# Retention and a GELU layer on one core: two chunks per group of small matmuls, and the tails turned by DMA

## The chip, the cores and the metric

One core of a Trainium2 chip runs the kernel. The metric is the device time of one execution in microseconds (us); several executions are taken and their median is compared. The engines have short names in the profile: PE is TensorE (PEld its weight loads), DVE is VectorE, ACT is ScalarE, POOL is GpSimd, and SP is the engine that issues most DMAs here.

## What is computed

There are 8 batches, 8 heads, a sequence of 576 positions and a head width of 64; the layer after it has 4608 rows, 512 inputs and 2048 hidden columns.

```
scores = scale * q @ k^T
Dmat   = gamma[h] ** (i - j) where i >= j, else 0
attn   = (scores * Dmat) @ v
x      = attn as [batch * 576, 8 * 64]
h      = x @ w_in
g      = 0.5 * h * (1 + tanh(c * (h + 0.044715 * h**3)))
out    = g @ w_out
```

Inputs and output are fp32; the kernel multiplies in fp16 and sums in fp32.

## The kernel before

**Retention by chunks.** The decay lets the sequence be cut into 4 chunks of 128 positions and a tail of 64 (called chunk `NC` in the code). For one chunk of one batch PE does the following small jobs. `score` (L304, matmul on L313) makes keys times queries, head by head: 8 matmuls that use 64 of the 128 rows of the array, two of them beside each other; VectorE multiplies the two PSUM banks that result by the causal mask (L319) into `ret`. `state` (L328, L333) makes keys times values, 8 matmuls that use 64 of the 128 columns, two beside each other; VectorE carries the running state on in `scan` (L341) and ScalarE spreads it into block form in `spread` (L351, L354). `av` (L356, L363) makes `ret` times values, again on 64 columns, and adds the part that comes from the chunks before (L381; for a tail L373) on the whole array. `put` (L389) copies the result to `xT` on ScalarE. Chunk 0 has no earlier part. A tail has its heads packed in two halves of the partitions, so it has half as many matmuls.

**The layer.** Rows are handled in 9 stages t of 512 rows: stages 0 to 7 have the four chunks of batch t, stage 8 all tails. From stage 2 on a stage has 30 steps u. Steps 0 to 15 are the up steps (`up`, L403: 4 matmuls of 128x512 and a GELU on ScalarE, through the two `hp` banks). After steps 3, 7, 11 and 15 VectorE makes sums of GELU results (`act_sums`, L480 to L483). Steps 16 to 29 are the product steps: seven products of half size, 1, 6, 5, 7, 2, 3 and 4 in this order, two steps each (`prod`, L485, matmul on L498), with their own banks A, B and C. After each product `after` (L505) adds or copies: product 6 leaves bank B, VectorE makes `u2` from it (L531), and product 7 then goes on summing into the same bank B; in the same way product 3 goes on in bank C once VectorE has read it (L536). Stage 1 has the same 30 steps with up steps in halves.

**Who decides the order.** The program is written in the order in which each engine executes it. `at(t, u, f)` hangs a job behind step u of stage t, and `run` emits it there. So every engine is a queue in program order; an instruction that waits holds back all behind it on its engine.

**Where the small jobs hang before.** `group` (L666) puts the score and the state of one chunk and the values (`av`) of the chunk before behind one step, and `PLAN` (L620) sets the steps: 6, 11, 16 and 21 for the four chunks of batch t+1, and 26 for the tail of batch t-2. Each group thus changes the way in which PE's array is split: whole, 64 rows, 64 columns, whole.

**Turning.** Scores need queries and keys with the head width on the partitions. Up to batch 2 PE does this (`turn`, L275). From batch 3 on `turn_dma` (L293) has SP issue two DMA transposes for a batch, behind step 24 of stage b-2. Before them POOL casts 8 blocks (L253, behind steps 16 to 23), and POOL is held by a copy named `gate` (L704, behind step 16) until the stage's last sums are made. The tails are all turned on PE, 4 matmuls each, with a copy on VectorE (L288). Their loads go over POOL's queue (L83), their casts over POOL (keys, queries) and ScalarE (values, L240).

**PSUM.** Eight banks: two `hp`, the three `att` banks t0, t1, t2 in turn, and A, B, C, which the small jobs may use while the products leave them free.

Of the kernel before, what the change touches and what calls it, by code (L numbers as in the profile page):

```python
# [10 lines left out]
ALU = mybir.AluOpType  # L11
F32 = mybir.dt.float32
# [7 lines left out]
def kernel(  # L20
# [43 lines left out]
    def bank(tag, name, dt=F32):  # L64
        if tag == "att":
            tag = "t" + str(turns["n"] % 3)
            turns["n"] += 1
        return ps.tile([128, 512 if dt == F32 else 1024], dt, tag=tag, name=name, bufs=BUFS[tag])
# [235 lines left out]
    def score(b, c, tag="att"):  # L304
        a = att[b]
        n = HP if c < NC else 2
        w = 128 * n
        d, o = turned(b, c)
        st = [bank(x, "st") for x in (tag if isinstance(tag, tuple) else (tag, tag))]
        for p in range(n):  # L310
            for hl in range(2):
                r = slice(64 * hl, 64 * hl + 64)
                nc.tensor.matmul(  # L313
                    st[hl][:, 128 * p : 128 * p + 128], d[r, 0, o + p, :], tq(b, c, p)[r], start=True, stop=True
                )
        m = cm if c < NC else tm
        for hl in range(2):
            r = sb.tile([128, 512], F16, tag="ret", name="ret", bufs=5)
            nc.vector.tensor_tensor(  # L319
                out=r[:, 0:w], in0=st[hl][:, 0:w], in1=m.rearrange("p n i -> p (n i)"), op=ALU.mult  # L320
            )
            a["ret"][c, hl] = r

# [1 line left out]
        c = c % NC  # L325
        return slice(512 * c + 128 * p + 64 * hl, 512 * c + 128 * p + 64 * hl + 64)

    def state(b, c, tag="att"):  # L328
        a = att[b]
        us = bank(tag, "us")  # L330
        for p in range(HP):
            for hl in range(2):
                nc.tensor.matmul(  # L333
                    us[64 * hl : 64 * hl + 64, 64 * p : 64 * p + 64],
                    a["k"][:, col(c, p, hl)],
                    a["v"][:, col(c, p, hl)],
                    start=True, stop=True,
                )
        a["U"] = us

    def scan(b, c):  # L341
        a = att[b]
        uc = a.pop("U")[:, 0:256].rearrange("p (q d) -> p q d", d=64)
        if c > 0:
            s = sb.tile([128, HP, 64], F32, tag="vs", name="vs", bufs=2)
            nc.vector.tensor_tensor(out=s, in0=uc, in1=a["w"], op=ALU.add)
            uc = s
        a["w"] = w = sb.tile([128, HP, 64], F32, tag="ws", name="ws", bufs=2)
        nc.vector.tensor_tensor(out=w, in0=uc, in1=gt, op=ALU.mult)  # L349

    def spread(b, c, cp, hls=(0, 1)):  # L351
        for hl in hls:
            r = slice(64 * hl, 64 * hl + 64)
            cp(out=(tbd[b % 2][r, c, :, r] if c < NC - 1 else tbt[b % 4][r, :, r]), in_=att[b]["w"][r])  # L354

    def av(b, c, tag="att"):  # L356
        a = att[b]
        n = HP if c < NC else 2
        td = tbd[b % 2]
        xs = bank(tag, "xs")  # L360
        for p in range(n):
            for hl in range(2):
                nc.tensor.matmul(  # L363
                    xs[64 * hl : 64 * hl + 64, 128 * p : 128 * p + 128],
                    act_of(b, "v", c)[:, col(c, p, hl)],
                    a["ret"][c, hl][:, 128 * p : 128 * p + 128],
                    start=(p == 0), stop=True, skip_group_check=True,
                )
        if c == NC:
            for s in range(2):  # L370
                for u in range(2):
                    o = 128 * s + 64 * u
                    nc.tensor.matmul(  # L373
                        xs[:, o : o + 64],
                        tbt[b % 4][:, 2 * u + s, :],
                        tq(b, c, s)[:, 64 * u : 64 * u + 64],
                        start=False, stop=True, skip_group_check=True,
                    )
        elif c > 0:
            for p in range(HP):  # L380
                nc.tensor.matmul(  # L381
                    xs[:, 128 * p : 128 * p + 128],
                    td[:, c - 1, p, :],
                    tq(b, c, p),
                    start=False, stop=True, skip_group_check=True,
                )
        a["xs"] = xs

    def put(b, c):  # L389
        xs = att[b].pop("xs")  # L390
        if c == NC:
            nc.scalar.copy(
                out=xT[:, GM + b].rearrange("p (u s) t -> p s u t", u=2),
                in_=xs[:, 0:256].rearrange("p (s u t) -> p s u t", s=2, u=2),
            )
            return
        src = xs.rearrange("p (n g t) -> p g n t", n=HP, g=2)
        g0 = 8 * (b % 2) + 2 * c
        nc.scalar.copy(out=xT[:, g0 : g0 + 2], in_=src)  # L399
# [170 lines left out]
        "o": (nc.vector.tensor_copy,),  # L570
    }

    CH = range(NC + 1)

    def cc(b, key, c, eng):
        cast(b, key, c, eng)
        pump(int(c < NC))
# [18 lines left out]

    def first(c):
        score(0, c, ST[c % 2])
        state(0, c, ("A", "t2")[c % 2])
        scan(0, c)  # L600

    first(0)
    for c in range(NC):
        if c + 1 < NC:
            cc(0, "k", c + 1, P)
            cc(0, "v", c + 1, P)
            turn(0, c + 1, A.copy, "C")
            spread(0, c, A.copy)
            filler(3, "B")
            first(c + 1)  # L610
        else:
            for g in range(4):
                for ct in range(4):
                    cast_w("i", g, ct)
            spread(0, c, A.copy)
            filler(3, "C")
        av(0, c, "B")
        put(0, c)

    PLAN = {1: zip((8, 13, 18, 23, 27), [(2, c) for c in range(NC)] + [()])}  # L620
    for t in range(2, 7):
        PLAN[t] = zip((6, 11, 16, 21, 26), [(t + 1, c) for c in range(NC)] + [(t - 2, NC)])
    PLAN[7] = zip((2, 7, 12, 17), [(5, NC), (6, NC), (7, NC), ()])
    TAILS = {b: ((b + 2, 5), (b + 2, 15)) for b in range(5)}
    TAILS |= {5: ((6, 16), (6, 24)), 6: ((6, 25), (7, 4)), 7: ((7, 5), (7, 9))}
    gate = const.tile([128, 1], F16, name="gate")
    events = {}

    def at(t, u, f):
        events.setdefault((t, u), []).append(f)  # L630

    def run(t, u):
# [20 lines left out]
    for c in range(NC):  # L653
        at(*CU[c], lambda c=c: (cc(1, "k", c, P), cc(1, "v", c, A if c else P)))
        at(*TU[c], lambda c=c: turn(1, c, A.copy))
        at(*VU[c], lambda c=c: (av(1, c, "AB"[c] if c < 2 else "att"), put(1, c), spread(1, c, A.copy)))
    for c in range(NC):
        at(*SU[c], lambda c=c: (score(1, c), state(1, c), scan(1, c)))
    at(1, 9, lambda: weight_sums(4, "32"))
# [1 line left out]
    at(1, 20, lambda: weight_sums(4, "4"))  # L661


    late = []

    def group(t, u, b=None, c=0):  # L666
        prev = late.pop() if late else None
        if b is not None:
            if b < NPE or c == NC:
                at(t, u - 2, lambda: turn(b, c, V.tensor_copy))  # L670
            at(t, u, lambda: score(b, c))
            if c < NC:
                at(t, u, lambda: (state(b, c), scan(b, c)))
                at(t, u + 2, lambda: spread(b, c, A.copy, (0,)))
                at(t, u + 3, lambda: spread(b, c, A.copy, (1,)))
            late.append((b, c))
        if prev:
            at(t, u, lambda: av(*prev, "C" if u < NF else "hp"))
            at(t, u + 1, lambda: put(*prev))

    def tail_in(t, u, b):
        at(t, u, lambda: load_tail(b))

    def tail_cast(t, u, b):
        at(t, u, lambda: (new_tail(b), [cc(b, key, NC, e) for key, e in zip("kqv", (P, P, A))]))

    for b, (l, k) in TAILS.items():
        tail_in(*l, b)
        tail_cast(*k, b)
    for t, us in PLAN.items():  # L690
        for u, x in us:
            group(t, u, *x)

    for b in range(2, B):
        ent = [(key, c) for c in range(NC) for key in "kqv"]
        eng = {"k": P, "q": P, "v": A}
        if b == 2:
            t0, ut = 1, [1, 1, 2, 6, 6, 7, 11, 11, 12, 16, 16, 17]
        else:
            t0, ut = b - 2, [16, 16, 17, 18, 18, 19, 20, 20, 21, 22, 22, 23]  # L700
        at(t0, ut[0], lambda b=b: (new_casts(b), new_turned(b)))
        if b >= HOLD:
            at(t0, ut[0], lambda: q_ld.update(hold=True))
            at(t0, ut[0], lambda t=t0: nc.gpsimd.tensor_copy(out=gate, in_=gs[t]["4"][:, NH - 1, 1, 0:1]))  # L704
        for u, (key, c) in zip(ut, ent):
            at(t0, u, lambda b=b, key=key, c=c, e=eng[key]: cc(b, key, c, e))
        if b >= NPE:
            at(t0, ut[-1] + 1, lambda b=b: turn_dma(b))
# [69 lines left out]
```

## Time and profile before

| | |
|---|---|
| median of 11 runs | 311.33 us (310.05 to 312.85) |
| the profiled execution | 311.8 us, of which the span from first to last instruction is 310.1 us |
| PE busy | 298.2 us, 96% of the span, mean granted clock 0.997 |
| DVE, ACT, POOL busy | 181.9, 170.6, 121.7 us |
| stage 1, stage 2 (start to start) | 37.1, 31.9 us |
| stages 3 to 6, each | 31.4 us: 15.8 up steps and 15.6 product steps |
| stage 7; stage 8 to its last matmul | 29.2; 26.6 us |
| PE waiting | 2.3 us before its first matmul, then 0.7 us for a DMA transpose in stage 2, 0.5 us for DVE in stage 8, and smaller ones in stages 0 and 1 |

Stage borders are read where PE's matmuls change from L498 to L409. A matmul's own time in the list of groups (379 ns for 128x512) contains its way through the array; the next one starts earlier, so work on PE is measured from start to start.

### The profile page before, as it was taken

What the parts mean: (1) busy time and instruction counts of PE and PEld (TensorE: products, weight loads), DVE (VectorE), ACT (ScalarE), POOL (GpSimd) and SP (SyncE); (2) the same over time, 40 slices, a digit from 0 to 9 for tenths busy, and PEclk for the clock granted to TensorE, in tenths of its full rate; (3) what the DMA queues carried; (4) which work ended last, traced back from release to release, by engine and by line L of the source; (5) the groups of instructions that cost most, each with busy time, mean ns of one, the idle gap of its engine ahead of it and who ended that gap; (6) DMA issues with size and microseconds to landing.
All of it is one profiled execution on the core that took longest, in us unless ns stands there. A gap on an engine that the chain in (4) does not pass through costs nothing.

```text
span 310.1 us, 6884 instructions
## 1 busy us (share of the span) xinstructions
PE 298.2 (96%) x2779; PEld 199.7 (64%) x2779; DVE 181.9 (59%) x368; ACT 170.6 (55%) x327; POOL 121.7 (39%) x177
## 2 busy tenths in 40 slices
PE   7889999799999999999999999999999999999994
PEld 3458655588884488447854785478547854784583
DVE  7651857779953766476637673776377545522431
ACT  6566417777645763577457645675466346406600
POOL 7678224640881069105910592049561430000000
PEclk9999999999999999999999999999999999999998
DMA  7999999999999994996499849933940040003004
GB/s 197 217 318 377 385 266 225 219 239 242 214 172 162 218 272 101 218 213 208 81 223 209 218 75 167 219 136 68 230 114 17 19 173 0 2 0 135 2 0 135
DMA packets 125983, 51.82 MB, mean 167 GB/s; under 512 B 114176, under 2 KB 116736, under 8 KB 125952
## 3 DMA queue, kind: packets, MB, share of 16 engines
q1 hardware_dynamic: 123936, 47.72, 71.7%
q0 software_dynamic: 1536, 3.15, 4.5%
q10 hardware_dynamic: 480, 0.52, 0.5%
q8 instruction: 21, 0.34, 0.5%
q14 instruction: 10, 0.08, 0.1%
HBM read 36.70 MB, written 9.44 MB: 149 GB/s over the span
## 4 chain that ended last, share of the span: by engine, by line
PE 76%; DMA 8%; SPq 4%; POOL 4%; issue 4%; DVE 2%; ACT 1%; POOLq 0%; DVEq 0%
PE hp L409 30%; PE opB L498 12%; PE opC L498 8%; PE opA L498 8%; PE hp L426 4%; PE op L445 4%; DMA tt<-cq 3%; DMA ld<-in_q_dram 3%; SPq L95 3%; PE st L313 3%; PE xs L363 2%; POOL cq L253 2%; DMA ld<-in_moe_w_in_dram 2%; PE us L333 2%; PE xs L381 2%
## 5 line engine op out<-in xcount | busy, mean ns | idle before, releaser
L409 PE MATMUL hp<-xT,w_in_sb 128*128 128x512 f16 x448 | 101.4, 379 | 0.0
L415 ACT ACTIVATE gT<-hp 128x512 f16<-128x512 f32 x112 | 66.8, 597 | 50.9 <-PE hp L409 50.3
L409 PEld LDWEIGHTS <-w_in_sb 128*128 128x128 f16 x448 | 42.6, 98 | 49.1 <-issue 2.9
L319 DVE TENSOR_TENSOR ret<-st,cm 128x512 f16<-128x512 f32 x64 | 41.2, 685 | 22.6 <-PE st L313 22.3
L498 PEld LDWEIGHTS <-gT 128*128 128x128 f16 x512 | 49.3, 98 | 7.5 <-issue 0.7
L253 POOL TENSOR_TENSOR ck<-ld,sc 128x512 f16<-128x512 f32 x31 | 34.8, 1123 | 22.1 <-DMA ld<-in_k_dram 22.1
L498 PEld LDWEIGHTS <-s 128*128 128x128 f16 x384 | 37.2, 98 | 4.2
L480 DVE TENSOR_TENSOR s<-gT 128x512 f16<-128x512 f16 x32 | 14.8, 462 | 40.8 <-ACT gT L415 39.9
L426 PE MATMUL hp<-xT,w_in_sb 128*128 128x256 f16 x256 | 30.3, 273 | 2.7 <-DVE ost L450 1.6
L498 PE MATMUL opA<-w_out_sb,gT 128*128 128x256 f16 x256 | 32.4, 273 | 0.0
L498 PE MATMUL opB<-wt,gT 128*128 128x256 f16 x256 | 30.7, 273 | 0.5 <-DVE ost L512 0.5
L704 POOL COPY gate<-s 128x1 f16<-128x1 f16 x5 | 0.9, 188 | 71.5 <-DVE s L483 71.5
L426 PEld LDWEIGHTS <-w_in_sb 128*128 128x128 f16 x256 | 24.5, 98 | 6.5 <-issue 2.6
L253 POOL TENSOR_TENSOR cq<-ld,sc 128x512 f16<-128x512 f32 x24 | 26.0, 1084 | 1.5 <-DMA ld<-in_q_dram 1.3
L399 ACT CAST xT<-xs 128x512 f16<-128x512 f32 x32 | 18.8, 586 | 12.5 <-PE xs L381 11.8
L432 ACT ACTIVATE gT<-hp 128x512 f16<-128x512 f32 x32 | 19.1, 597 | 9.0 <-PE hp L426 8.9
L354 ACT CAST tbd<-ws 64x256 f16<-64x256 f32 x48 | 19.3, 403 | 5.9 <-DVE ws L349 5.2
L240 ACT CAST cv<-ld 128x512 f16<-128x512 f32 x27 | 16.2, 619 | 1.7 <-DMA ld<-in_v_dram 1.4
L512 DVE TENSOR_TENSOR k<-k,opB 128x512 f32<-128x512 f32 x16 | 10.9, 683 | 10.2 <-PE opB L498 10.1
L512 DVE TENSOR_TENSOR ost<-k,opC 128x512 f32<-128x512 f32 x16 | 11.0, 687 | 9.6 <-PE opC L498 9.4
L498 PE MATMUL opC<-w_out_sb,s 128*128 128x256 f16 x128 | 16.1, 273 | 0.0
L349 DVE TENSOR_TENSOR ws<-vs,gt 128x256 f32<-128x256 f32 x24 | 15.3, 637 | 1.2
(97 smaller groups left out, 375.7 us busy)
## 6 DMA issues: line engine op xcount, KB each, us to landing
ld<-in_q_dram SPq DMA_DIRECT2D x32, 256.0 KB, 5.2
ld<-in_k_dram SPq DMA_DIRECT2D x32, 256.0 KB, 5.2
ld<-in_v_dram SPq DMA_DIRECT2D x32, 256.0 KB, 5.1
out_dram<-ost SPq DMA_DIRECT2D x16, 512.0 KB, 4.8
ld<-in_moe_w_in_dram SPq DMA_DIRECT2D x16, 256.0 KB, 5.7
ld<-in_moe_w_out_dram SPq DMA_DIRECT2D x16, 256.0 KB, 5.6
lt<-in_k_dram POOLq DMA_DIRECT2D x16, 64.0 KB, 4.5
lt<-in_q_dram POOLq DMA_DIRECT2D x16, 64.0 KB, 4.1
```

The source lines that it names most:

```text
L240: eng.copy(out=dst, in_=raw)
L253: eng.tensor_tensor(out=dst.rearrange("p (h d) -> p h d", d=D), in0=raw.rearrange("p (h d) -> p h d", d=D), in1=sc[:, s0 : s0 + nh].unsque ...
L319: nc.vector.tensor_tensor(out=r[:, 0:w], in0=st[hl][:, 0:w], in1=m.rearrange("p n i -> p (n i)"), op=ALU.mult)
L349: nc.vector.tensor_tensor(out=w, in0=uc, in1=gt, op=ALU.mult)
L354: cp(out=(tbd[b % 2][r, c, :, r] if c < NC - 1 else tbt[b % 4][r, :, r]), in_=att[b]["w"][r])
L399: nc.scalar.copy(out=xT[:, g0 : g0 + 2], in_=src)
L409: nc.tensor.matmul(hp.rearrange("p (g t) -> p g t", t=TL), w_in_sb[:, ct, 128 * fc : 128 * fc + 128], xT[:, o : o + TB // TL, ct, :], star ...
L415: nc.scalar.activation(out=gT[t][:, fc].rearrange("p i n -> p (i n)"), in_=hp, func=AF.Gelu_apprx_tanh)
L426: nc.tensor.matmul(hp[:, 256 * x : 256 * x + 256].rearrange("p (g t) -> p g t", t=TL), w_in_sb[:, ct, 128 * (f + x) : 128 * (f + x) + 128] ...
L432: nc.scalar.activation(out=gT[t][:, f : f + 2, 2 * u : 2 * u + 2, :].rearrange("p f i n -> p f (i n)"), in_=hp.rearrange("p (f n) -> p f n ...
L498: nc.tensor.matmul(op[tag][:, HD * u : HD * u + HD], lhs(f), rhs[:, f], start=(new and u == 0 and f == 0), stop=(f == NH - 1), skip_group_ ...
L512: nc.vector.tensor_tensor(out=o, in0=a, in1=b, op=ALU.add)
```

## The change

From batch 2 on one event holds one kind of job for two chunks. Behind one step PE does both chunks' scores (four banks, with a tail's scores behind them); behind another both states in one bank and then the values of two chunks and of a tail, all on 64 columns, followed by the parts from earlier chunks, all on the whole array. In stages 3 to 6 these are steps 6 (scores of chunks 0 and 1 and of the tail of batch t-3), 12 (states of 2 and 3, values of 0, 1 and the tail), 17 (scores of 2 and 3) and 24 (states of chunks 0 and 1 of the batch after, values of 2 and 3). The two scores at step 6 use t0, t1, t2 and A, the tail B and C; at step 17 the second chunk uses both `hp` banks. Stage 7 holds the last four tails in two events each for scores and values. In stage 1 the chunks of batch 2 are turned behind steps 7, 9, 15 and 18 instead of 6, 11, 16 and 21.

The tails are turned by two DMA transposes each on SP's queue (16 in all) instead of 4 matmuls and a copy on VectorE. The cast of a tail's values on ScalarE moves from step 15 to step 14 in the stages that carry batches 0 to 4. The buffers of `ret` go from 5 to 4, with 2 half-size ones for tails.

The core of the diff (`av` is also cut into `av` and `inter`, which holds the part from earlier chunks, and `state` takes a bank and a half of it):

```
-    PLAN = {1: zip((8, 13, 18, 23, 27), [(2, c) for c in range(NC)] + [()])}
-    for t in range(2, 7):
-        PLAN[t] = zip((6, 11, 16, 21, 26), [(t + 1, c) for c in range(NC)] + [(t - 2, NC)])
-    PLAN[7] = zip((2, 7, 12, 17), [(5, NC), (6, NC), (7, NC), ()])
-    TAILS = {b: ((b + 2, 5), (b + 2, 15)) for b in range(5)}
+    TAILS = {b: ((b + 2, 5), (b + 2, 14), (b + 2, 14)) for b in range(5)}
...
+    def scores(t, u, *xs):
+        at(t, u, lambda: [score(*x) for x in xs])
+
+    def states(t, u, b, c, tag):
+        def go():
+            us = bank(tag, "us")
+            for n in range(2):
+                state(b, c + n, us, n)
+            for n in range(2):
+                scan(b, c + n)
+        at(t, u, go)
+        def sp(n, hl):
+            at(t, u + 2 + 2 * n + hl, lambda: spread(b, c + n, A.copy, (hl,)))
+        for n in range(2):
+            for hl in range(2):
+                sp(n, hl)
+
+    def values(t, u, *xs):
+        at(t, u, lambda: ([av(*x) for x in xs], [inter(*x[:2]) for x in xs]))
+        for n, x in enumerate(xs):
+            at(t, u + 1 + n, lambda x=x: put(*x[:2]))
+
+    def turn_tail(b, k):
+        def go():
+            for y, key in enumerate("kq"):
+                nc.sync.dma_start_transpose(out=att[b]["ett"][:, y], in_=att[b]["e" + key])
+        at(k[0], k[1] + 3, go)
...
+        if t == 1:
+            for c, (u, tag) in enumerate(((7, "t2"), (9, "A"), (15, "C"), (18, "hp"))):
+                turns_of(t, u, b, c, tag)
+            u0, u1, u2, u3 = 11, 17, 21, 26
+            states(t, u0, b, 0, "B")
+            scores(t, u0, (b, 0, ("t0", "t1")), (b, 1, ("t2", "A")))
+        else:
+            u0, u1, u2, u3 = (8, 14, 19, 25) if t == 2 else (6, 12, 17, 24)
+            tail = [(e, NC, ("B", "C"))] if e >= 0 else []
+            scores(t, u0, (b, 0, ("t0", "t1")), (b, 1, ("t2", "A" if t > 2 else "C")), *tail)
+        states(t, u1, b, 2, "t0")
+        values(t, u1, (b, 0, "t1"), (b, 1, "t2"), *([(e, NC, "B")] if e >= 0 else []))
+        scores(t, u2, (b, 2, ("t1", "t2")), (b, 3, ("hp", "hp")))
+        if t < 6:
+            states(t, u3, b + 1, 0, "t0")
+        values(t, u3, (b, 2, "t1"), (b, 3, "t2"))
+    for n, u in enumerate((7, 21)):
+        x, y = (4 + 2 * n, NC), (5 + 2 * n, NC)
+        scores(7, u, x + (("t0", "t1"),), y + (("hp", "hp") if n else ("t2", "A"),))
+        values(7, u + 4, x + ("t2" if n else "B",), y + ("t0" if n else "C",))
```

In the loop b is t+1 and e is t-3.

More of the change, by code (lines that the diff above doesn't have):

```diff
@@ L317, in score @@
         for hl in range(2):
-            r = sb.tile([128, 512], F16, tag="ret", name="ret", bufs=5)
+            tag, n = ("ret", 4) if c < NC or b in (5, 7) else ("rett", 2)
+            r = sb.tile([128, 512 if tag == "ret" else 256], F16, tag=tag, name=tag, bufs=n)[:, 0:w]
             nc.vector.tensor_tensor(
-                out=r[:, 0:w], in0=st[hl][:, 0:w], in1=m.rearrange("p n i -> p (n i)"), op=ALU.mult
+                out=r, in0=st[hl][:, 0:w], in1=m.rearrange("p n i -> p (n i)"), op=ALU.mult
             )
@@ L326, in col, with state @@
         return slice(512 * c + 128 * p + 64 * hl, 512 * c + 128 * p + 64 * hl + 64)
-    def state(b, c, tag="att"):
+    def state(b, c, us=None, n=0):
         a = att[b]
-        us = bank(tag, "us")
+        us = bank("att", "us") if us is None else us
         for p in range(HP):
@@ L333, in state @@
                 nc.tensor.matmul(
-                    us[64 * hl : 64 * hl + 64, 64 * p : 64 * p + 64],
+                    us[64 * hl : 64 * hl + 64, 256 * n + 64 * p : 256 * n + 64 * p + 64],
                     a["k"][:, col(c, p, hl)],
@@ L338, in state @@
                 )
-        a["U"] = us
+        a["U", c] = us[:, 256 * n : 256 * n + 256]
     def scan(b, c):
         a = att[b]
-        uc = a.pop("U")[:, 0:256].rearrange("p (q d) -> p q d", d=64)
+        uc = a.pop(("U", c)).rearrange("p (q d) -> p q d", d=64)
         if c > 0:
@@ L347, in scan @@
             uc = s
-        a["w"] = w = sb.tile([128, HP, 64], F32, tag="ws", name="ws", bufs=2)
+        a["w"] = a["w", c] = w = sb.tile([128, HP, 64], F32, tag="ws", name="ws", bufs=2)
         nc.vector.tensor_tensor(out=w, in0=uc, in1=gt, op=ALU.mult)
@@ L353, in spread @@
             r = slice(64 * hl, 64 * hl + 64)
-            cp(out=(tbd[b % 2][r, c, :, r] if c < NC - 1 else tbt[b % 4][r, :, r]), in_=att[b]["w"][r])
+            cp(out=(tbd[b % 2][r, c, :, r] if c < NC - 1 else tbt[b % 4][r, :, r]), in_=att[b]["w", c][r])
     def av(b, c, tag="att"):
@@ L358, in av @@
         n = HP if c < NC else 2
-        td = tbd[b % 2]
-        xs = bank(tag, "xs")
+        a["xs", c] = xs = bank(tag, "xs")
         for p in range(n):
@@ L368, in av, with inter @@
                 )
+    def inter(b, c):
+        xs = att[b]["xs", c]
         if c == NC:
@@ L382, in av @@
                     xs[:, 128 * p : 128 * p + 128],
-                    td[:, c - 1, p, :],
+                    tbd[b % 2][:, c - 1, p, :],
                     tq(b, c, p),
@@ L386, in av @@
                 )
-        a["xs"] = xs
     def put(b, c):
-        xs = att[b].pop("xs")
+        xs = att[b].pop(("xs", c))
         if c == NC:
@@ L571 @@
     }
-    CH = range(NC + 1)
     def cc(b, key, c, eng):
@@ L598, in first @@
         score(0, c, ST[c % 2])
-        state(0, c, ("A", "t2")[c % 2])
+        state(0, c, bank(("A", "t2")[c % 2], "us"))
         scan(0, c)
@@ L617 @@
         av(0, c, "B")
+        inter(0, c)
         put(0, c)
-    PLAN = {1: zip((8, 13, 18, 23, 27), [(2, c) for c in range(NC)] + [()])}
-    for t in range(2, 7):
-        PLAN[t] = zip((6, 11, 16, 21, 26), [(t + 1, c) for c in range(NC)] + [(t - 2, NC)])
-    PLAN[7] = zip((2, 7, 12, 17), [(5, NC), (6, NC), (7, NC), ()])
-    TAILS = {b: ((b + 2, 5), (b + 2, 15)) for b in range(5)}
-    TAILS |= {5: ((6, 16), (6, 24)), 6: ((6, 25), (7, 4)), 7: ((7, 5), (7, 9))}
+    TAILS = {b: ((b + 2, 5), (b + 2, 14), (b + 2, 14)) for b in range(5)}
+    TAILS |= {5: ((6, 15), (6, 24), (6, 24)), 6: ((6, 25), (7, 4), (7, 12)), 7: ((7, 5), (7, 13), (7, 13))}
     gate = const.tile([128, 1], F16, name="gate")
@@ L629, in at @@
     def at(t, u, f):
+        if t > 0 and u > 29:
+            t, u = t + 1, u - 30
         events.setdefault((t, u), []).append(f)
@@ L655 @@
         at(*TU[c], lambda c=c: turn(1, c, A.copy))
-        at(*VU[c], lambda c=c: (av(1, c, "AB"[c] if c < 2 else "att"), put(1, c), spread(1, c, A.copy)))
+        at(*VU[c], lambda c=c: (av(1, c, "AB"[c] if c < 2 else "att"), inter(1, c), put(1, c), spread(1, c, A.copy)))
     for c in range(NC):
@@ L661 @@
     at(1, 20, lambda: weight_sums(4, "4"))
[L664 to L692, printed above, removed]
+    def scores(t, u, *xs):
[13 more added lines that the diff above has]
+                sp(n, hl)
@@ new lines, in values, with turns_of @@
+    def values(t, u, *xs):
[7 more added lines that the diff above has]
+        at(k[0], k[1] + 3, go)
+    def turns_of(t, u, b, c, tag):
+        at(t, u, lambda: turn(b, c, V.tensor_copy, tag))
@@ new lines @@
+    for b, (l, k, v) in TAILS.items():
+        at(*l, lambda b=b: load_tail(b))
+        at(*k, lambda b=b: (new_tail(b), [cc(b, key, NC, P) for key in "kq"]))
+        at(*v, lambda b=b: cc(b, "v", NC, A))
+        turn_tail(b, k)
+    for t in range(1, 7):
+        b, e = t + 1, t - 3
+        if t == 1:
[14 more added lines that the diff above has]
+        values(t, u3, (b, 2, "t1"), (b, 3, "t2"))
@@ L697 @@
         if b == 2:
-            t0, ut = 1, [1, 1, 2, 6, 6, 7, 11, 11, 12, 16, 16, 17]
+            t0, ut = 1, [1, 1, 2, 4, 4, 5, 9, 9, 10, 13, 13, 14]
         else:
```

## The prediction

> **What bounds it.** I read the engines' busy times and the chain first: PE works through nearly the whole span, and the chain that ended last is PE's, so time is saved by giving PE less to do and lost where PE waits.
>
> ```profile
> PE 298.2 (96%) x2779; PEld 199.7 (64%) x2779; DVE 181.9 (59%) x368; ACT 170.6 (55%) x327; POOL 121.7 (39%) x177
> ...
> PE 76%; DMA 8%; SPq 4%; POOL 4%; issue 4%; DVE 2%; ACT 1%; POOLq 0%; DVEq 0%
> ```
>
> Then PE's timeline (start, length, line). Only the starts count, since matmuls overlap.
>
> ```profile
> 155.69 6.25 PE L409 MATMUL hp<-xT,w_in_sb 128*128 128x512 f16 x28
> 161.87 0.40 PE L313 MATMUL st<-tt 64*128 64x128 f16 x8
> 162.20 0.32 PE L333 MATMUL us<-cv,ck 128*64 128x64 f16 x8
> 162.35 0.28 PE L363 MATMUL xs<-ret,ev 128*64 128x128 f16 x4
> 162.56 0.29 PE L373 MATMUL xs<-ett,tbt 128*128 128x64 f16 x4
> ...
> 172.94 0.39 PE L363 MATMUL xs<-ret,cv 128*64 128x128 f16 x8
> 173.27 0.40 PE L381 MATMUL xs<-tt,tbd 128*128 128x128 f16 x4
> ```
>
> Four pairs of L363 take 0.33 us until the next kind starts (172.94 to 173.27), two pairs 0.21 (162.35 to 162.56): so a pair costs 0.06, and 0.09 remains that no matmul fills. Single starts in the trace say the same: 0.095 us is lost whenever PE's array goes from whole to 64 rows, to 64 columns, or back, and nothing where the split stays (L333 to L363). Work alone: a chunk's score 0.23, states 0.13, values 0.23, part from before 0.22; a tail's 0.11, 0.11, 0.12.
>
> **What PE is spared.** Switches of split: before, 14 in stage 1, 15 each in stages 2 to 6, 11 in stage 7: 100. After: 9, 8 each, 8: 57. 43 x 0.095 = 4.1 us, all on the path. The tails' 32 transposes go; in the trace they follow each other by 0.056: 1.8 us. Here the skill (TensorE: Matmul & The Clock Gate, Part 4: PE-mode transpose) says about 275 ns each in a kernel; that would be 8.8 us. The row lists 219 ns, but that is a latency which the next one overlaps, so I take 1.8. In stage 2 PE waited 0.66 for the transposes of batch 3; their scores go from step 6 to 8, 1.7 us later, so the wait goes. The up steps of stages 3 to 6 take 15.81: 64 x 0.216 = 13.82, the two groups 1.8, and 0.15 to 0.2 of small waits, where copies put GELUs late. The change leaves steps 0 to 12 free of such copies: 0.15 in 6 stages, 0.9. Sum 7.5.
>
> **What PE will wait for.** The rule against this change is in TensorEngine Tiling (Array Packing), PSUM Bottleneck: tiling speeds the matmuls, not the emptying of PSUM. Were that the bound throughout, the 4.1 us would be worth nothing. By stage DVE is busy 8.8 of 15.8 us in up steps and 10.3 of 15.6 in product steps, so I charge the rule only where a matmul needs a bank that DVE is late with. There is such a place in stages 3 to 6:
>
> ```profile
> 172.59 0.43 DVE L480 TENSOR_TENSOR s<-gT 128x512 f16<-128x512 f16 x1 [1.47 <-ACT gT L415]
> ...
> 174.06 1.28 DVE L319 TENSOR_TENSOR ret<-st,cm 128x512 f16<-128x512 f32 x2
> ...
> 176.66 0.68 DVE L512 TENSOR_TENSOR k<-k,opB 128x512 f32<-128x512 f32 x1
> ```
>
> S is the start of product 1 (171.50 here). The last four sums start at S+1.09, when the last GELU ends. After: four masks follow them at once, then the `u2` that frees bank B for product 7. ScalarE first. From step 12 on its queue holds GELU 13, put, GELU 14, cast of the tail's values, spread, put, GELU 15. Starts follow each other as in this view: put after GELU 0.50, GELU after put 0.46, spread after GELU 0.64, GELU after spread 0.31 to 0.43.
>
> ```profile
> 169.51 0.58 ACT L399 CAST xT<-xs 128x512 f16<-128x512 f32 x1
> 169.97 0.62 ACT L415 ACTIVATE gT<-hp 128x512 f16<-128x512 f32 x1
> 170.61 0.41 ACT L354 CAST tbd<-ws 64x256 f16<-64x256 f32 x1
> 170.92 0.58 ACT L415 ACTIVATE gT<-hp 128x512 f16<-128x512 f32 x1
> ```
>
> A GELU can start 1.07 after its step does. Steps 13 to 15 start at S-2.59, S-1.73, S-0.86, so GELU 13 starts at S-1.52; put, GELU 14, cast, spread, put follow, and GELU 15 starts at S+1.2 and ends at S+1.8. Sums: 1.85 to 3.3. Masks every 0.60: S+3.3 to 5.7. `u2` ends at S+6.4. PE reaches product 7 after six half products (6 x 0.873) and the two scores (0.65): S+5.9. It waits 0.55, and with it all behind it in its queue, four times: 2.2 us (bounds: 0, if DVE gets to the masks at S+1.1 as before, and 4, if GELU 15 is 0.45 later still). Stage 2 escapes: its values stand at step 14 and its scores at 19, behind `u2`.
>
> Stage 1 has two such places; the sizes are those of its DVE rows. Until step 6 (65.7) nothing changes. The four sums after step 7 end at 70.2 as before; then two sums of weights (0.69 each) and the copy of chunk 1 of batch 2 (0.68) end at 72.2. PE, with two turns of 0.45 and five steps of 0.87 behind it, wants the scores at 71.3: 0.9. In the product steps weights 1.28, two scans (2.1 while POOL casts), a copy 0.68, `u2` 0.67, weights 0.93, four masks 2.4 and two adds of 0.69 stand, 9.4 in all, between the last sums (79.3) and the end of the read of bank C (88.7), which product 3 wants at 87.7: 0.9 to 1.0. Together 1.8; between 0.5 and 3.
>
> POOL's gate is as late as the sums, and behind it in turn stand POOL's casts, SP's big transposes, and PE's scores of the next stage (views of POOL, SP and PE):
>
> ```profile
> 174.28 0.19 POOL L704 COPY gate<-s 128x1 f16<-128x1 f16 x1 [16.24 <-DVE s L483]
> ```
>
> ```profile
> 183.80 5.24 SPq L296 DMA_TRANSPOSE tt<-cq  x1
> ```
>
> ```profile
> 193.28 0.40 PE L313 MATMUL st<-tt 64*128 64x128 f16 x8
> ```
>
> The gate falls at S+2.8, the eight casts end at 182.8 (8.5 later), the queries' transpose is issued at S+12.3. The trace puts the landings of batches 4 to 7 at 128.6, 159.9, 193.1, 223.8, and PE's scores at 130.5, 161.9, 193.3, 224.7: slack 1.9, 2.0, 0.2, 0.9. After, gate and transposes are 0.76 later after S (not for batch 4), and the scores, at S+21.8 before, come at S+14.2 (14 half products 12.2; at step 17 0.65; at step 24 states 0.26, values 0.46, parts 0.44, two switches 0.19) + 0.55 + 6.2 (seven up steps and a switch) = S+21.0. Slack shrinks by 1.6: waits of about 0, 0, 1.4, 0.7; with the mean landing time, 8.3 after issue, 0.4 each. I take 1.5; bounds 0 and 4.4 (each as slow as batch 6, 9.3).
>
> **Edits at no cost.** The tails' 16 DMA transposes stand on SP's queue, where SP lay idle from 172.5 to 181.85 before the big ones; behind them are the big transposes, then loads and stores. The trace has none that small. Near row: 512 KB take 1.9 to 5.5 us of SP and land after 4.3 or more. An eighth of that is 0.2 to 0.7; as dear as the large ones, a pair is 7 us, still inside 9.3. I take 0; a gain isn't possible, for nothing waits for SP then, and the saved PE time is counted above. In stage 7 the last four wait for PE's values of step 11 and have 8.7 us until the scores at step 21; with 5 for the landing there is cover, if each took 2 us to issue PE would wait 4. Keys and queries of a tail are cast as soon as they have landed, ten steps ahead. The cast of its values now stands before GELU 15, but its load is issued by 186.4 and lands 5.3 later, seven steps ahead; late, it would hold up GELU 15 one for one. States at step 24 need casts that end at S+6.9; PE is there at S+8.5. Stores wait on SP for nothing new. Eight copies of 0.42 leave DVE, hidden anyway. Fewer `ret` buffers: each four are read before the next four are written.
>
> **Sum.** 7.5 - 2.2 - 1.8 - 1.5 = 2.0. On the profiled execution (311.8, span 310.1): 309.8. That execution lies 0.5 above the median of 311.33, so the median goes to 309.3.
>
> **Rivals.** *ScalarE's copies don't overlap* (slower): if put, cast and spread take their full 0.58 and 0.41, GELU 15 ends 0.45 later. Each 0.1 of that costs 0.1 in four waits for `u2` and in up to three landings: 7 x 0.45 = 3.2, giving 312.5. It turns the sign at 0.3. For it: the queue has three copies more between GELUs 13 and 15 than any in the trace; against: the starts above. *Landings bind* (no change): all transposes as late as batch 6's cost 2.9 more: 312.2; with half of that, 310.8. For it: batch 3 took even 10.1; against: batches 4 and 5. *The waits don't come* (faster still): PE's spared 7.5 less half of the costs, 306.5; everything, 303.8. For it: DVE has 5 us idle per half stage; against: program order.
>
> **Chances.** Forecast 0.47, faster still 0.15, landings 0.17, ScalarE 0.21. What a measurement can tell from no change is 0.3%, 0.9 us: faster 0.62, same 0.17, slower 0.21. The range, 306.3 to 312.6, takes in half the waits on one side and either rival on the other.
>
> **What would show it.** Right: stages 3 to 6 near 30.9; PE waiting on L514 (DVE, bank B) by about 0.5 in each of them; stage 2 near 30.0, stage 1 near 38.4; scores of batches 6 and 7 waiting for a DMA transpose. Wrong: GELU 15 ending after S+2.2, PE waiting for `ett`, or product 7 not waiting at all.

## The result and the profile after

The changed kernel takes 308.63 us (median of 13 runs, 307.11 to 310.2). Against the runs of the kernel before made beside it (311.17) the ratio is 0.9918, 95% interval 0.9898 to 0.9938: faster by 2.5 us. The profiled execution took 309.4 us with a span of 307.7.

The busy times and the chain that ended last, in the same order as before:

```profile
PE 293.1 (95%) x2747; PEld 198.4 (64%) x2747; DVE 177.7 (58%) x360; ACT 168.7 (55%) x327; POOL 120.0 (39%) x177
...
PE 72%; DVE 13%; ACT 6%; SPq 4%; DMA 2%; issue 2%; POOL 0%; DVEq 0%
```

PE lost 5.1 us of busy time and 32 matmuls (the tails' turns). It still carries the chain, but DVE's share rose from 2% to 13% and ScalarE's from 1% to 6%: the chain now runs through places where PE waits for the other two.

Stages, start to start, from PE's timeline (up steps + product steps). E1 is the changed kernel run again.

| stage | before | after | E1 |
|---|---|---|---|
| 1 | 21.02 + 16.06 | 22.13 + 17.05 | 20.51 + 17.02 |
| 2 | 16.31 + 15.60 | 15.91 + 14.26 | 15.91 + 14.26 |
| 3 | 15.81 + 15.60 | 16.19 + 14.74 | 16.18 + 14.75 |
| 4 | 15.81 + 15.60 | 16.01 + 14.74 | 16.00 + 14.75 |
| 5 | 15.81 + 15.60 | 16.00 + 14.75 | 16.00 + 14.75 |
| 6 | 15.81 + 15.60 | 16.00 + 15.21 | 16.28 + 15.22 |
| 7 | 16.50 + 12.69 | 15.15 + 13.35 | 15.14 + 13.35 |
| last matmul starts at | 305.74 | 303.33 | 302.23 |

The 22.13 of stage 1 belongs to this one execution: for 3.41 us from 57.6 on, at the end of a wait of 1.6 us for DVE, PE was granted half its clock. Busy times by stretch show it (the columns are PE, PEld, DVE, ACT, POOL, each with its instructions, then the granted clock, DMA share and GB/s); first the profiled execution of the changed kernel, then E1's:

```profile
58.00:62.00 4.00, 4.00 (x32) 2.94 (x31) 1.99 (x4) 1.55 (x3) 2.49 (x3) 0.63 1.35 222
```

```profile
58.00:62.00 4.00, 4.00 (x56) 3.14 (x55) 1.86 (x5) 3.08 (x7) 2.34 (x4) 1.00 1.38 220
```

PE is busy for all 4.00 us in both, and starts 32 matmuls in one and 56 in the other. So stage 1 is compared by E1. Before and E1 differ by 3.5 us in the profiled executions (311.8, 308.3), of which some 0.8 is luck: the one lay 0.6 above its median, the other 0.2 below.

Stage 4 again, which the prediction worked through (S is the start of product 1; it is 171.50 here too). PE's timeline of the changed kernel:

```profile
171.50 1.91 PE L500 MATMUL opA<-w_out_sb,gT 128*128 128x256 f16 x16
173.34 0.62 PE L313 MATMUL st<-tt 64*128 64x128 f16 x16
174.11 1.91 PE L500 MATMUL opB<-wt,s 128*128 128x256 f16 x16 [0.15 <-ACT xT L394]
175.85 1.91 PE L500 MATMUL opC<-wt,s 128*128 128x256 f16 x16
177.88 0.71 PE L500 MATMUL opB<-wt,gT 128*128 128x256 f16 x5
```

The scores of two chunks stand in one row of 16. Product 6 waits 0.15 for the tail's put, and product 7 comes 2.03 after product 5, where 5 came 1.74 after 6: 0.28 late. (From start to start the wait of product 6 costs 0.22: it follows the start of the scores by 0.77, in E6 below, where nothing waits, by 0.55.) DVE and ScalarE show why:

```profile
173.28 0.43 DVE L482 TENSOR_TENSOR s<-gT 128x512 f16<-128x512 f16 x1 [2.52 <-ACT gT L417]
...
174.76 2.48 DVE L320 TENSOR_TENSOR ret<-st,cm 128x512 f16<-128x512 f32 x4
177.15 0.68 DVE L514 TENSOR_TENSOR k<-k,opB 128x512 f32<-128x512 f32 x1
```

```profile
171.57 0.41 ACT L240 CAST ev<-lt 128x256 f16<-128x256 f32 x1
171.88 0.40 ACT L355 CAST tbd<-ws 64x256 f16<-64x256 f32 x1
172.19 0.57 ACT L401 CAST xT<-xs 128x512 f16<-128x512 f32 x1
172.66 0.59 ACT L417 ACTIVATE gT<-hp 128x512 f16<-128x512 f32 x1
173.28 0.40 ACT L355 CAST tbd<-ws 64x256 f16<-64x256 f32 x1
173.69 0.37 ACT L394 CAST xT<-xs 128x256 f16<-128x256 f32 x1
```

Cast, spread and put stand ahead of the last GELU (172.66 to 173.25); DVE waits 2.52 us for that GELU, then does sums, four masks and `u2` (177.15 to 177.83), and product 7 starts 0.05 later. The tail's put, last of these rows, ends at 174.06 and lets product 6 go.

Three waits in PE's list that were not there before (us in all, times, longest); the 0.7 for `tt<-cq` is gone from it:

```profile
PE opC L500 <- DVE ost L514: 1.0, 1, 1.0
PE opB L500 <- DVE k L514: 0.8, 1, 0.8
...
PE opB L500 <- ACT xT L394: 0.6, 4, 0.2
```

The first is stage 1's, the second stage 6's (1.0 from start to start), the third is 0.15 in each of stages 3 to 6. The 0.28 of stages 3 to 5 is not in the list and is read from the starts.

### The profile page after: what moved, and what is told of

The parts are those of the page before. It is cut to its first block, busy times and chain, and to the rows that moved or that the text cites. A ratio compares the mean times of both kernels' runs of the same rounds, so it can differ in the third digit from the quotient of the medians.

```text
span 307.7 us, 6860 instructions
## 1 busy us (share of the span) xinstructions
PE 293.1 (95%) x2747; PEld 198.4 (64%) x2747; DVE 177.7 (58%) x360; ACT 168.7 (55%) x327; POOL 120.0 (39%) x177
## 4 chain that ended last, share of the span: by engine, by line
PE 72%; DVE 13%; ACT 6%; SPq 4%; DMA 2%; issue 2%; POOL 0%; DVEq 0%
PE hp L411 30%; PE opB L500 11%; PE hp L428 8%; PE opC L500 6%; PE opA L500 6%; DVE ret L320 5%; PE op L447 4%; SPq L95 3%; PE xs L363 2%; ACT gT L417 2%; DMA ld<-in_moe_w_in_dram 2%; PE xs L384 2%; PE st L313 2%; PE us L334 1%; DVE wt L471 1%
## 5 line engine op out<-in xcount | busy, mean ns | idle before, releaser
L411 PEld LDWEIGHTS <-w_in_sb 128*128 128x128 f16 x448 | 42.9, 98 | 50.1 <-issue 2.2
L320 DVE TENSOR_TENSOR ret<-st,cm 128x512 f16<-128x512 f32 x64 | 40.0, 683 | 10.2 <-PE st L313 10.1
L253 POOL TENSOR_TENSOR ck<-ld,sc 128x512 f16<-128x512 f32 x31 | 33.5, 1081 | 21.1 <-DMA ld<-in_k_dram 21.1
L428 PE MATMUL hp<-xT,w_in_sb 128*128 128x256 f16 x256 | 31.3, 280 | 2.7 <-DVE ost L452 1.6
L500 PE MATMUL opA<-w_out_sb,gT 128*128 128x256 f16 x256 | 31.2, 273 | 0.0
L428 PEld LDWEIGHTS <-w_in_sb 128*128 128x128 f16 x256 | 25.2, 100 | 6.7 <-issue 2.4
L544 ACT COPY ost<-opA 128x512 f32<-128x512 f32 x8 | 4.7, 585 | 44.0 <-PE opA L500 36.4
L514 DVE TENSOR_TENSOR k<-k,opB 128x512 f32<-128x512 f32 x16 | 10.9, 683 | 16.4 <-PE opB L500 16.4
L500 PE MATMUL opC<-w_out_sb,s 128*128 128x256 f16 x128 | 15.4, 273 | 1.0 <-DVE ost L514 1.0
L500 PE MATMUL opB<-wt,s 128*128 128x256 f16 x128 | 15.4, 272 | 0.6 <-ACT xT L394 0.6
```

The source lines that it names most:

```text
L253: eng.tensor_tensor(out=dst.rearrange("p (h d) -> p h d", d=D), in0=raw.rearrange("p (h d) -> p h d", d=D), in1=sc[:, s0 : s0 + nh].unsque ...
L320: nc.vector.tensor_tensor(out=r, in0=st[hl][:, 0:w], in1=m.rearrange("p n i -> p (n i)"), op=ALU.mult)
L411: nc.tensor.matmul(hp.rearrange("p (g t) -> p g t", t=TL), w_in_sb[:, ct, 128 * fc : 128 * fc + 128], xT[:, o : o + TB // TL, ct, :], star ...
L428: nc.tensor.matmul(hp[:, 256 * x : 256 * x + 256].rearrange("p (g t) -> p g t", t=TL), w_in_sb[:, ct, 128 * (f + x) : 128 * (f + x) + 128] ...
L500: nc.tensor.matmul(op[tag][:, HD * u : HD * u + HD], lhs(f), rhs[:, f], start=(new and u == 0 and f == 0), stop=(f == NH - 1), skip_group_ ...
L514: nc.vector.tensor_tensor(out=o, in0=a, in1=b, op=ALU.add)
```

## The experiments

All are the changed kernel with one edit, run beside the kernel before; each ratio is to that.

**E1, the changed kernel again.**

> The changed kernel itself, beside its variants on one chip. Both theories: about 308.6 us, 0.992 of the time before. Its first profile had a stretch of 3.4 us at half clock in stage 1; if that belongs to the change it is there again, if not the up steps of stage 1 take about 21.1 us instead of 22.1.

308.49 us, 0.9907 (0.9878 to 0.9937). Its trace has no half clock in stage 1, and up steps of 20.51 there. It is the base of what follows.

**E2, the scores of two chunks behind two steps** (in stages 2 to 6).

```
-  scores(t, u0, (b, 0, ...), (b, 1, ...), *tail)
+  scores(t, u0, (b, 0, ...))
+  scores(t, u0 + 1, (b, 1, ...), *tail)
...
-  scores(t, u2, (b, 2, ...), (b, 3, ...))
+  scores(t, u2, (b, 2, ...))
+  scores(t, u2 + 1, (b, 3, ...))
```

> In stages 2 to 6 the scores of the second chunk (and of the tail with it) hang one step later than those of the first, so that the two are no longer neighbours; all else is the same. Theory (each change of PE's split costs 0.095 us): two more switches at each of two places in five stages, 20 x 0.095 = 1.9 us slower than the changed kernel, each such stage longer by 0.38. Rival (the gain comes from waits and queues, not from switches): no difference, or a small gain because DVE gets its banks one after the other.

310.14 us, 0.9957 (0.9941 to 0.9974), 1.65 more than E1. The up steps of stages 2 to 6 grow by 0.21 to 0.22 (in stage 6 against the 16.00 of the profiled execution), two switches each. The product steps grow by 0.21 in stage 2, by 0.16 in stages 3 to 5 and by nothing in stage 6, where PE would have waited for bank B anyway. A switch costs 0.105 to 0.11, and less where a wait stands behind it.

**E3, the tails turned by PE.**

```
-  turn_tail(b, k)
+  at(*PT[b][:2], lambda b=b: turn(b, NC, V.tensor_copy, PT[b][2]))
```

> The grouping stays, the tails are turned on PE again (4 matmuls and a copy on DVE each, two steps before their scores). Theory: 32 x 0.056 = 1.8 us slower than the changed kernel, 0.22 in each of stages 3 to 6 and 0.9 in stage 7, less what stage 6 gets back (there POOL's tail casts ran beside DVE's sums, 0.5). Rival [...]: 7 to 8.8 us slower.

309.45 us, 0.9951 (0.9931 to 0.9971), 0.96 more than E1. Up steps +0.23 in each of stages 3 to 6 (stage 6 against the 16.00 again), +0.44 in both halves of stage 7: 1.8 for 32 transposes, 0.056 each. The rival, that a transpose costs PE the 219 ns of its row or the 275 ns that the prediction weighed, fell. Back came 0.73 in the product steps of stage 6 (14.49 for 15.22), more than the 0.5 that had been read from what POOL does there. The view of POOL, first before, then after the change:

```profile
244.80 0.61 POOL L253 TENSOR_TENSOR ek<-lt,sc 128x256 f16<-128x256 f32 x1 [7.48 <-PE tr L283]
245.37 0.61 POOL L253 TENSOR_TENSOR eq<-lt,sc 128x256 f16<-128x256 f32 x1
```

```profile
233.76 1.22 POOL L83 DMA_DIRECT2D lt<-in_v_dram  x2 [3.53 <-ACT ev L240]
234.99 0.69 POOL L253 TENSOR_TENSOR ek<-lt,sc 128x256 f16<-128x256 f32 x1
235.65 0.79 POOL L253 TENSOR_TENSOR eq<-lt,sc 128x256 f16<-128x256 f32 x1
```

Before, these casts (keys and queries of the tail of batch 6) waited for PE's turn of an older tail to free their buffer. A DMA transpose frees it earlier, and the casts fall beside DVE's last sums:

```profile
234.78 0.44 DVE L482 TENSOR_TENSOR s<-gT 128x512 f16<-128x512 f16 x1 [2.52 <-ACT gT L417]
235.25 0.72 DVE L483 TENSOR_TENSOR s<-s,gT 128x512 f16<-128x512 f16 x1
235.90 0.83 DVE L484 TENSOR_TENSOR gT<-gT 128x512 f16<-128x512 f16 x1
236.65 0.41 DVE L485 TENSOR_TENSOR s<-gT,s 128x512 f16<-128x512 f16 x1
```

Two sums take 0.72 and 0.83 where they take 0.42 alone: 0.71 more, and so much later come the masks, `u2` and product 7. In E3's trace the casts wait for PE again, until 252.36.

**E4, stage 1's sums of weights behind step 24.**

```
-  at(1, 20, lambda: weight_sums(4, "4"))
+  at(1, 24, lambda: weight_sums(4, "4"))
```

> The last sum of weights in stage 1 moves from step 20 to step 24, behind the read of bank C. Theory (product 3 of stage 1 waits for DVE's queue): its wait of 1.04 us goes, 1.0 us faster than the changed kernel. Rival (the wait only moves to the next bank or to the masks): less than 0.3 us.

307.49 us, 0.9876 (0.9834 to 0.9918). The product steps of stage 1 take 16.08 instead of 17.02 (E1) or 17.05 (the profiled execution), and the wait for `ost` on bank C is gone: it cost 0.94 to 0.97. The intervals of E4 and E1 overlap, so the gain is read from the traces and not from the medians.

**E5, the second scores two steps later**, so that product 7 comes after more of PE's work.

```
-  u0, u1, u2, u3 = (8, 14, 19, 25) if t == 2 else (6, 12, 17, 24)
+  u0, u1, u2, u3 = (8, 14, 19, 25) if t == 2 else (6, 12, 19, 24)
```

> In stages 3 to 6 the second pair of scores hangs behind step 19 instead of 17, so that DVE reads bank B for product 7 before the four masks. Theory (program order on DVE makes product 7 wait): the waits of 0.28 us in stages 3 to 5 and 1.0 in stage 6 go, 1.8 us faster than the changed kernel, unless the scores of batch 6, whose transpose landed only 0.2 us ahead, take up to 0.1 to 0.3 of it back. Rival (the wait moves on to bank C or to the values at step 24): less than 0.5 us.

309.17 us, 0.9916 (0.9888 to 0.9944): the expected gain did not come. Product steps of stages 3 to 5 went from 14.75 up to 15.13, those of stage 6 from 15.22 down to 14.87. Of the waits on PE:

```profile
PE opB L500 <- ACT xT L394: 2.8, 4, 0.7
```

Four waits of 0.7 in place of 0.15. Product 7 no longer waits for `u2`, but PE reaches product 6 one pair of scores (0.55) earlier, and bank B still holds the tail's values, whose put stands behind GELU 15 on ScalarE. So the wait moved from product 7 to product 6. The theory that only DVE's order (masks ahead of `u2`) makes PE wait fell here: ScalarE is late too, and the scores had covered it.

**E6, ScalarE relieved ahead of GELU 15**: the cast of the tail's values goes from step 14 to 17, and the first spread one step back, both behind that GELU.

```
-  TAILS = {b: ((b + 2, 5), (b + 2, 14), (b + 2, 14)) for b in range(5)}
+  TAILS = {b: ((b + 2, 5), (b + 2, 14), (b + 2, 17)) for b in range(5)}
...
-  at(t, u + 2 + 2 * n + hl, lambda: spread(b, c + n, A.copy, (hl,)))
+  at(t, u + 2 + 2 * n + hl + (t > 2 and u == 12 and n == 0 and hl == 0), lambda: spread(b, c + n, A.copy, (hl,)))
```

> In stages 3 to 6 two copies on ScalarE move behind GELU 15 (the cast of the tail's values to step 17, the first spread from step 14 to 15). Theory (ScalarE's backlog sets when the last sums start): the last GELU ends about 0.6 us earlier after S, gate and bank B come 0.6 earlier, product 7 no longer waits in stages 3 to 5 and 0.4 less or more in stage 6; 1.2 to 1.5 us faster than the changed kernel. Rival (DVE's own work is what is late): GELU earlier, the wait unchanged, no gain.

305.54 us, 0.9809 (0.9768 to 0.9849). Stage 4 in its trace (S = 169.37), DVE and PE:

```profile
170.43 0.43 DVE L482 TENSOR_TENSOR s<-gT 128x512 f16<-128x512 f16 x1 [1.79 <-ACT gT L417]
...
174.30 0.67 DVE L514 TENSOR_TENSOR k<-k,opB 128x512 f32<-128x512 f32 x1
```

```profile
171.76 1.92 PE L500 MATMUL opB<-wt,s 128*128 128x256 f16 x16
173.52 1.91 PE L500 MATMUL opC<-wt,s 128*128 128x256 f16 x16
175.26 1.91 PE L500 MATMUL opB<-wt,gT 128*128 128x256 f16 x16
```

Sums start at S+1.06 instead of S+1.78, `u2` ends at S+5.60 instead of S+6.33, and the products follow each other by 1.75 with no wait. Product steps: 14.26 in stages 3 to 5, 14.01 in stage 6. That is 0.49 three times and 1.2, 2.7 in all, about twice what was expected, because the put's waits and all of stage 6's went too. In stage 5 the scores of batch 6 waited 0.3 for their DMA transpose.

**E7, E4 and E5 together.**

> The last weight sum late and the second scores behind step 19 together. Theory: the two waits are in different stages, so the gains add: 2.8 us faster than the changed kernel, about 305.8 us, 0.983 of the time before. Rival: the second one only brings PE to the landing of the big transposes earlier and gives half back: 307.

307.92 us, 0.9875 (0.9847 to 0.9904). Stage 1 gains its 0.97 (16.08); product steps of stages 3 to 5 stay at 15.1. The 305.8 that was expected rested on the theory that E5 refuted.

**E8, E4 and E6 together.**

> Both edits that paid by themselves: ScalarE's cast of the tail's values and its first spread go behind GELU 15, and stage 1's sums of weights from step 20 to 24. Theory: they take away waits in different stages, so they add. E6 was at 0.981 of before, E4 took 0.97 us more from stage 1 (product steps 17.05 to 16.08): 0.978, about 304.6 us, with product steps 16.1 in stage 1, 14.26 in stages 3 to 5, 14.0 in stage 6. Rival: PE now arrives at the scores of batches 5 to 7 before their DMA transposes have landed, and gives the gain back there: 305.5, up steps of stages 4 to 6 over 16.3 and waits of the scores for a DMA.

304.01 us, 0.9793 (0.9769 to 0.9818). Stage 1 has 16.08, stages 3 to 6 have 14.26 three times and 14.01: the gains add. It is faster than both kernels; before took 310.49 beside it. In this trace landings do not bind: transposes land at S+19.5 to 19.9, scores stand at S+20.4 to 20.6. That is no rule, for in E6 the landing of batch 6 came at S+20.6.

**E9, only the cast behind GELU 15** (the first edit of E6), and **E10, only the spread** (the second).

> The changed kernel with only the cast of the tail's values behind GELU 15 (the first spread stays ahead of it). Theory: GELU 15 and all behind it come one copy earlier, 0.31 us by the starts in the trace. In stages 3 to 5 PE waits 0.28 for u2 and 0.17 for the tail's put, so one copy less is nearly enough: product steps 14.3 there instead of 14.74, stage 6 about 0.3 shorter (14.9); sum -1.5, 306.9 us. Rival (the waits shrink in proportion, half of E6's gain for one of two copies): 14.5 in stages 3 to 5 and 14.6 in stage 6.

> The changed kernel with only the first spread behind GELU 15 (the cast stays ahead of it). Theory as for the cast alone: one copy of 0.40 us less ahead of GELU 15, whose starts are 0.30 apart, so product steps 14.3 in stages 3 to 5, 14.9 in stage 6, 306.9 us. Rival: the spread matters less, since it also waits for PE's states at step 12 and the cast, which waits for nothing, would only slide into its place: 14.6 to 14.7 and 308.

E9: 306.40 us, 0.9859 (0.9831 to 0.9887). E10: 307.95 us, 0.9914 (0.9891 to 0.9937). In stages 3 to 5 both have product steps of 14.44 to 14.45, not 14.3: either copy is worth 0.30, and 0.2 is left. But it is left in different places. PE in stage 4, E9 first, then E10:

```profile
171.74 0.62 PE L313 MATMUL st<-tt 64*128 64x128 f16 x16
172.29 1.92 PE L500 MATMUL opB<-wt,s 128*128 128x256 f16 x16
174.04 1.91 PE L500 MATMUL opC<-wt,s 128*128 128x256 f16 x16
175.97 1.91 PE L500 MATMUL opB<-wt,gT 128*128 128x256 f16 x16
```

```profile
172.16 0.62 PE L313 MATMUL st<-tt 64*128 64x128 f16 x16
172.91 1.91 PE L500 MATMUL opB<-wt,s 128*128 128x256 f16 x16
174.65 1.91 PE L500 MATMUL opC<-wt,s 128*128 128x256 f16 x16
176.40 1.91 PE L500 MATMUL opB<-wt,gT 128*128 128x256 f16 x16
```

In E9 product 7 comes 1.93 after product 5, so 0.18 of the wait for `u2` is left, and product 6 comes 0.55 after the scores began, without a wait. In E10 product 7 comes after 1.75, without a wait, and product 6 comes 0.75 after the scores began, 0.20 late: the late spread went ahead of the tail's put, which product 6 needs. So "nearly enough" was wrong, and so was E10's rival: cast and spread weigh the same in stages 3 to 5. The medians do not show E10's 0.9 (0.9914 against E1's 0.9907); in its trace stage 1 took 38.1 for E1's 37.5, and the scores waited 0.5 for transposes. In stage 6 E9 and E10 part, 14.18 and 15.21. DVE and POOL there, E9 first, then E10:

```profile
234.10 0.42 DVE L484 TENSOR_TENSOR gT<-gT 128x512 f16<-128x512 f16 x1
```

```profile
236.82 0.63 POOL L253 TENSOR_TENSOR ek<-lt,sc 128x256 f16<-128x256 f32 x1
```

```profile
234.46 0.83 DVE L484 TENSOR_TENSOR gT<-gT 128x512 f16<-128x512 f16 x1
```

```profile
234.22 0.78 POOL L253 TENSOR_TENSOR eq<-lt,sc 128x256 f16<-128x256 f32 x1
```

POOL's load of values waits for ScalarE's cast to free its buffer, and POOL's own casts stand behind that load. A late cast on ScalarE holds POOL off until DVE's sums are done (234.10 and 236.82 in E9); a late spread alone does not (234.46 and 234.22 in E10). This is the rest of E6's gain in stage 6.

E9 also shows the landings: in its stage 5 the scores waited.

```profile
191.36 0.62 PE L313 MATMUL st<-tt 64*128 64x128 f16 x16 [0.78 <-DMA tt<-cq]
```

## Why the prediction was right, and where its steps were not

The prediction had the sign and the size (309.3; measured 308.63). Its mechanism held, but the closeness of the sum is in part luck: several terms missed by 0.5 to 1.5 us, with opposite signs. Step by step:

- **Switches (4.1).** Right, and a little low. E2 put 20 back and paid 0.105 to 0.11 for each that no wait hid; 43 of these are 4.5.
- **Transposes (1.8).** Right, by the starts and not by the page: E3 puts 32 back for 1.8, 0.056 each. The 275 ns that the Trainium skill (TensorE: Matmul & The Clock Gate, Part 4: PE-mode transpose) gives would have been 8.8.
- **Stage 2 (0.66).** Right: no wait for `tt<-cq` there; the transpose of batch 3 landed at 100.17, the scores came at 102.54. Stage 2 takes 30.17 (predicted near 30.0).
- **Small waits of the GELUs (0.9).** Failed: nothing was gained. By the starts of PE's up matmuls these waits were 0.18 in each of stages 2 to 6 before and none in stage 7, 0.9 in all. After, they are 0.04 in stages 4 to 6, as predicted, but 0.29 in stage 2, 0.24 in stage 3 and 0.22 in stage 7: 0.87 in all. In stage 7 casts and puts of the tails stand between GELUs. The first steps of stages 2 and 3 are not free of copies, since spreads of the states behind step 26 or 25 of the stage before reach into them. ScalarE at the start of stage 3, where before no copy stood between the GELUs:

```profile
125.68 0.60 ACT L417 ACTIVATE gT<-hp 128x512 f16<-128x512 f32 x1 [2.42 <-PE hp L411]
126.30 0.40 ACT L355 CAST tbd<-ws 64x256 f16<-64x256 f32 x1
126.73 1.26 ACT L417 ACTIVATE gT<-hp 128x512 f16<-128x512 f32 x2
```

- **Wait for `u2` (0.55 each, 2.2).** Right in place, mechanism and size in stages 3 to 5, too small in stage 6. The times held: GELU 15 was to end at S+1.8 and did at S+1.75, `u2` at S+6.4 and did at S+6.33. Product 7 itself waited only 0.28, because product 6 had already been held for the tail's put on bank B, which the prediction left out. From start to start the two cost 0.22 + 0.28 = 0.50. Stage 6 it took as like the others, where 1.2 was lost because POOL's casts slowed DVE (E3, E9, E10). The four stages took 30.9, 30.8, 30.8 and 31.2, where 30.9 was forecast. E6 takes all of these waits away: 2.7. The rule it was weighed by (the Trainium skill, TensorEngine Tiling (Array Packing), PSUM Bottleneck: tiling does not speed the emptying of PSUM) bears on banks B and C alone, as assumed. At bank B it is not DVE's work alone that is late: ScalarE's queue ahead of GELU 15 sets when DVE starts (E5, E6).
- **Stage 1, bank C (0.9).** Right: 1.0 in the list of waits, 0.94 to 0.97 by E4.
- **Stage 1, copy of the turned chunk (0.9).** Too dear. In the traces of the changed kernel and its variants PE waited for that copy between 0 and 1.2, and the wait goes with another one at about 57 us, ahead of every edit: where PE waited 1.2 or 1.6 for DVE there, the copy cost 0 to 0.3 (after, E1, E4, E5, E9, E10); where 0.8, it cost 0.4 to 1.2 (E2, E3, E6, E7, E8). The kernel before had the 1.6 as well; its table of waits passes over it, though it is the longest after PE's first matmul. This may be one debt of DVE that PE pays sooner or later, but no run tests it, and the sum of the two waits still ranges from 1.2 to 2.0. Where the early wait was 1.6, as before, stage 1 takes 38.0 to 38.1 (E5, E9, E10), 0.3 to 0.4 less than the 38.4 forecast. E1's 37.5 had a shorter early wait.
- **Landings (1.5).** Failed in size: 0 in the profiled execution, 0.2 in E1, 0 to 0.9 in E2 to E10. The gate came as predicted (S+3.48 for S+3.54) and the scores too (S+20.92 for S+21.0), but the time from gate to landing was taken from before (18.8 for batch 6) and was 17.2. POOL's eight casts took 8.19 instead of 8.55, since two of them no longer took 1.22 but 1.04 like the rest (why is not shown), and the transposes themselves were faster. In the profiled execution 0.2 us of slack is left for batch 6; in E9 a landing 18.2 after the gate cost 0.78. So the mechanism exists, but the landing time of one execution was taken as the rule.
- **Tail transposes at no cost.** Right in the sum, wrong in the size. SP's view:

```profile
173.22 2.55 SPq L690 DMA_TRANSPOSE ett<-ek  x1
175.86 1.85 SPq L690 DMA_TRANSPOSE ett<-eq  x1
182.19 2.98 SPq L296 DMA_TRANSPOSE tt<-ck  x1
```

In this trace 64 KB take 1.2 to 2.6 us of SP, not 0.2 to 0.7, and 512 KB take 1.9 to 4.6: the time doesn't go with the bytes. (The large ones of before ranged from 1.3 to 5.5, not from 1.9.) A pair of tail transposes lies between the two bounds, and its cover was enough: in stage 4, 4.5 us still lie between the pair and the next transpose, and PE never waits for `ett`. What was missed is a cost elsewhere: the DMA transposes free the tail's buffers sooner, and in stage 6 POOL's casts thus fall beside DVE's sums (0.7, E3).

The sum. Counted from start to start and without waits, PE's work in stages 1 to 7 shrank by 6.5 to 6.6 (the profiled execution, E1), where switches and transposes were to give 5.9. With stage 2's 0.7 and nothing from the GELUs this is 7.3, close to the 7.5 predicted, but made up otherwise. Paid were 2.7 in stages 3 to 6, 1.0 to 1.2 in stage 1 and 0 to 0.3 for landings, 3.7 to 4.2 instead of 5.5. That leaves 3.1 to 3.6 by the stages where 2.0 was forecast. From stage 1 on, the profiled executions of before and E1 differ by 3.7, of which 0.4 is the shorter early wait of stage 1; the medians differ by 2.5 to 2.9. What of *the waits don't come* was true is the copy, in part, and the landings. *Landings bind* did not come as a whole. *ScalarE's copies don't overlap* fell: the starts were as read.

## What to carry to other kernels

Putting small jobs of one kind together is worth what the trace charges for each change of the array's split, but it bundles what the other engines get as well: follow each bank from its last writer through the engine that empties it to the next matmul, and look at every copy that stands ahead of the last one on that engine's queue. Here two copies moved behind one GELU and one sum of weights moved by four steps were worth 3.6 us by the stages (E8), about as much as the change itself. When copies are moved off a busy stretch, look at what stands where they land: here the GELUs of stages 2, 3 and 7 lost what those of stages 4 to 6 gained. And before a time seen once goes into a sum, see how far it varies: from the gate to the landing, batches 4 to 7 took 17.0 to 18.8 us in one execution of the kernel before.

## What the hardware showed that was not expected

- DVE's sums of fp16 tensors of 128x512 take 0.41 to 0.43 us without a cast of POOL beside them (1,281 of 1,282 in the twelve traces from 95 us on), and up to 0.86, once 1.22, where a cast overlaps them by more than 0.2. In the views of stage 6 above, POOL's casts of 128x256 take 0.61 to 0.63 otherwise and 0.69 to 0.79 beside the sums.
- In the traces of the changed kernel and its variants, the two large transposes of batch 6 take 9.5 to 10.9 us together (SP's time for the keys' issue, and from the queries' issue to their landing), however the two parts fall (1.32 + 8.22, 2.98 + 6.95): a long issue is followed by a short landing.
- PE ran at half clock for 3.41 us in stage 1 in two of eleven traces of the changed kernel and its variants (after, E4), each time at the end of a wait of PE of 1.6 us. With the same wait, before, E5, E9 and E10 did not. What decides stays open.
